# One core, three chained layers: the right-hand tiles of the last layer begin 352 bytes lower

## The chip, the cores and the metric

The kernel runs on one core of one Trainium2 chip. The metric is the device time of one execution in microseconds. All times below are of the kernel before the change.

## The reference

Three layers follow one another. The first is attention with the delta rule (4 batches, 8 heads, 768 tokens, head size 48): a state of 48x48 for each head is read and updated token by token. Its output, turned to 3072 tokens by 384, goes through two feed-forward layers. What matters here is the last one.

```
def _moe_ref(x, w_in, w_out):            # layer 1: 384 -> 2048 -> 384
    h = np.maximum(x @ w_in, 0.0)
    return h * h @ w_out
def _moe2_ref(x, w_gate, w_val, w_out):  # layer 2: 384 -> 1536 -> 384
    gate = 1.0 / (1.0 + np.exp(-(x @ w_gate)))
    val = x @ w_val
    return gate * val @ w_out
```

All data are 32-bit floats. The kernel keeps the precision with split operands: each number is a high part and a low part, and each product is three matmuls (high x high, low weight x high, high weight x low).

## The kernel before, in words

**Order of the work.** Attention and layer 1 are interleaved by a list of steps written out by hand (`ORDER`); every engine runs its instructions in the order in which the program issues them, and the framework adds the waits. Layer 1 makes `h` from `xhi`, `xlo` with the weights `w1h` (high, kept in SBUF) and `il` (low, fetched for each step) in line 681, and adds to `o` in line 719 with `gh`, `gl`. The tokens go in six groups of 512 columns, so the matmuls of both layers have 128 rows, 128 weights and 512 columns.

**Layer 2.** Three pairs of groups are handled together by a scheme that needs fewer products (11 instead of 12 for a pair of groups and a pair of hidden blocks). For each pair there are 12 halves: six pairs of hidden blocks, each for `gate` and for `val`. One half has seven pieces (`PIECES`), each of three or six matmuls that add up in one PSUM tile `gx` or `gy` (line 1138). Their weights come from `wg`; their moving operands are ten blocks of tokens or of sums of tokens: three of them lie in `xhi`, `xlo`, seven in `xa` (first and third pair) or `xb` (second pair). VectorE adds every piece to `gateA` to `gateD` or `valA` to `valD` (line 1052), ScalarE copies the first piece (line 1142) and takes the sigmoid, and VectorE multiplies `gate` by `val` (line 1063). The products are split into `gh`, `gl` (or `p` tiles), and their matmuls with `wo` into `o` (line 1019) are put between the pieces. The last group's output is made at the end in line 1197, with the hidden values as weights and `wo` as the moving operand, 384 columns.

**What is prepared on the way.** During the end of layer 1 and the first pair, VectorE, ScalarE and GpSimd convert raw weights (`raw2`, `y2`, lines 792 to 809), make sums of weights (`wr`, line 859) and split them into `wg` (lines 867, 872) and `wo` (lines 880, 884); token sums come from `x2r` and `xt` (lines 914 to 926).

**Where the tiles lie.** SBUF is given out from two sides. On the left lie `work` (`xhi`, `xlo`, `gg`, `gh`, `gl`, `p`), the weights of layer 1 and, once these are closed, `w2y`: eight of the twelve blocks of `wo` (f from 4 to 11), `xb`, `obt`, and the `gate` and `val` tiles. All of these begin at 128 modulo 512 bytes of the partition. On the right lay the tiles of attention; when they are closed, the pool `w2x` takes their place: `xa`, `x2r`, `xt`, `raw2`, `y2`, the first four blocks of `wo`, and `wr`, `wor`, `wg`. A pool on the right ends at the top of SBUF and its tiles lie upward from its base in the order in which they are made. A column slice of a moving operand is 2048 bytes and one of the weights 512 bytes, and the tiles are multiples of 512 bytes, so every operand of layer 2 has the place modulo 512 of the tile that it is in.

Of the kernel before, what the change touches and what calls it, by code (L numbers as in the profile page):

```python
# [7 lines left out]
F32 = mybir.dt.float32  # L8
# [83 lines left out]
def kernel(  # L92
# [681 lines left out]
    with tc.manual_schedule():  # L774
# [39 lines left out]
        assert not (z_t or kn_t or v_t or q_t or pm_t or N_t or xr_t or yt_t or o_t)  # L814
        at.close()
        w2x = ctx.enter_context(tc.tile_pool(name="w2x", bufs=1, side="right", reuse_waits="tile"))
        w2x.tile([128, 24], F32, name="pad")
        xa_t = w2x.tile([128, 2, 7, GT], F32R, name="xa")
        x2r_t = w2x.tile([128, 2, KD, GT], F32, tag="x2r", name="x2r")
        xt_t = w2x.tile([128, GT], F32, name="xt")  # L820
# [189 lines left out]
        def o_product(g, f, m, i, start, stop):  # L1010
            if start:
                po2[g, m] = (
                    ps_o.tile([128, GT], F32, tag=f"o{m}", name=f"o{m}") if g % 2 == 0
                    else ps_2.tile([128, GT], F32, tag=f"o{m + 3}", name=f"o{m + 3}")
                )
            hi, lo = (w[:, m * 128:m * 128 + 128] for w in wo_t[f])
            ph, pl = p_t[g, f]
            w, x = ((hi, ph), (lo, ph), (hi, pl))[i]
            nc.tensor.matmul(out=po2[g, m], lhsT=w, rhs=x, start=start, stop=stop)  # L1019
# [60 lines left out]
        for hh in range(halves):  # L1080
# [87 lines left out]
            if v:  # L1168
                assert not queue
                for k, (g, f) in enumerate(((g0, fo), (g0, fe), (g0 + 1, fe), (g0 + 1, fo))[:4 if g0 + 2 < NG else 2]):  # L1170
                    for m in range(KD):
                        for r in range(3):
                            queue.append([
                                lambda g=g, f=f, m=m, r=r, a=j == 0 and k % 2 == 0 and r == 0, z=j == NP - 1 and k % 2 and r == 2:
                                o_product(g, f, m, r, bool(a), bool(z)), None])
                    if j == NP - 1 and k % 2:
                        queue[-1][1] = g
        while after:
            k = min(after)
            for fn in after.pop(k):  # L1180
                step[0] = k
                fn()
# [114 lines left out]
```

## Time and profile before

| | |
|---|---|
| median of three runs | 1065.0 us |
| the three runs | 1072.24, 1065.0, 1062.05 us |
| the profiled execution | 1069.8 us, span 1068.1 us |
| granted TensorE clock, mean over the span | 0.99 |
| first matmul of layer 2 (line 1138) | 632.9 us |
| last matmul of line 1138 and line 1019 | 1033.5 and 1038.2 us |
| last stage (line 1197) | 1038.5 to 1063.8 us |

The span runs from the first to the last instruction; the time of the execution has 1.7 us more around it. Layer 2 and the last stage take the last 435 us of it. The number after the duration of a matmul in a row is its count; matmuls overlap, so their distance from start to start is shorter than their duration.

### The profile page before, as it was taken

Reading aid. Unit: us, or ns where it says so; the run is one execution under the profiler, and the core shown is the slowest. Engines: PE = TensorE matmul, PEld = TensorE weight load, DVE = VectorE, ACT = ScalarE, POOL = GpSimd, SP = SyncE. Lnnn points to the kernel's source line nnn. Section 1 sums busy time; section 2 is a strip of 40 time slices with the busy share of each in tenths; the row PEclk is TensorE's granted clock in tenths of the full one; section 3 lists DMA queues with packets and bytes.
Section 4 is the critical chain, followed back from the end, with each engine's and each line's share of the span. In section 5 each row is a group of like instructions: output and inputs, shape, how many; then the busy total and the mean of one; then the engine's idle time right before and its main releaser. Section 6 shows DMA issues by size and latency. Waiting matters only on the chain.

```text
span 1068.1 us, 27414 instructions
## 1 busy us (share of the span) xinstructions
PE 1001.8 (94%) x11611; PEld 819.5 (77%) x11611; DVE 763.3 (71%) x1436; ACT 458.4 (43%) x763; POOL 233.9 (22%) x181
## 2 busy tenths in 40 slices
PE   4575999999999999999999999999999999999998
PEld 2564777777787887788788887787888888878888
DVE  6979889868788874974344768988676566676770
ACT  2343665454554555445555745434322332222220
POOL 4352444200011101010011015668601221000000
PEclk9998999999999999999999999999999999999999
DMA  9666666675685856665547766644644332244302
GB/s 268 187 211 171 219 200 196 215 201 148 166 217 146 243 169 197 173 187 174 149 150 248 245 214 242 219 157 149 231 144 133 102 121 88 91 135 160 117 1 60
DMA packets 81803, 182.78 MB, mean 171 GB/s; under 512 B 22032, under 2 KB 54928, under 8 KB 77072
## 3 DMA queue, kind: packets, MB, share of 16 engines
q1 hardware_dynamic: 81392, 180.76, 55.2%
q8 instruction: 91, 1.49, 0.6%
q10 hardware_dynamic: 288, 0.26, 0.1%
q14 instruction: 32, 0.26, 0.1%
HBM read 139.30 MB, written 36.96 MB: 165 GB/s over the span
## 4 chain that ended last, share of the span: by engine, by line
PE 82%; DVE 4%; DMA 4%; issue 2%; SPq 1%; ACT 1%; DVEq 0%; ACTq 0%
PE h L681 17%; PE o L719 17%; PE gx L1138 12%; PE gy L1138 12%; PE o L1019 11%; PE r L1197 2%; DMA il<-w1d 2%; PE att L553 1%; PE att L584 1%; PE att L620 1%; PE att L622 1%; PE att L566 1%; PE att L377 1%; PE att L538 1%; PE att L363 1%
## 5 line engine op out<-in xcount | busy, mean ns | idle before, releaser
L704 DVE TENSOR_TENSOR gl<-gg,gh 128x512 fp32r<-128x512 f32 x96 | 72.8, 765 | 88.4 <-ACT gg L698 87.9
L695 ACT ACTIVATE gg<-h 128x512 f32<-128x512 f32 x96 | 57.4, 598 | 177.8 <-PE h L681 170.8
L719 PE MATMUL o<-gh,il 128*128 128x512 f32 x288 | 112.7, 391 | 1.0 <-DMA il<-w1d 1.0
L1019 PE MATMUL o<-gh,wo 128*128 128x512 f32 x270 | 93.1, 395 | 0.0
L681 PE MATMUL h<-xhi,il 128*128 128x512 f32 x288 | 84.5, 402 | 4.6 <-issue 2.7
L719 PE MATMUL o<-gh,w1h 128*128 128x512 f32 x216 | 86.9, 402 | 0.0
L719 PE MATMUL o<-gl,w1h 128*128 128x512 f32 x216 | 84.3, 390 | 0.0
L1138 PE MATMUL gy<-xa,wg 128*128 128x512 f32 x288 | 76.4, 394 | 0.3
L1138 PE MATMUL gx<-xa,wg 128*128 128x512 f32 x288 | 76.5, 394 | 0.0
L681 PEld LDWEIGHTS h<-xhi,il 128*128 128x128 f32 x288 | 55.3, 193 | 18.6 <-issue 3.6
L168 POOL TENSOR_TENSOR y<-raw 128x768 f32<-128x768 f32 x12 | 19.7, 1644 | 220.1 <-DVE raw L161 195.7
L681 PE MATMUL h<-xhi,w1h 128*128 128x512 f32 x216 | 65.7, 413 | 0.0
L1138 PEld LDWEIGHTS gy<-xa,wg 128*128 128x128 f32 x288 | 53.9, 188 | 13.5 <-DVE gateB L1052 0.6
L1138 PEld LDWEIGHTS gx<-xa,wg 128*128 128x128 f32 x288 | 53.9, 188 | 13.2 <-DVE gateB L1052 0.5
L719 PEld LDWEIGHTS o<-gh,il 128*128 128x128 f32 x288 | 54.1, 188 | 12.3 <-DMA il<-w1d 1.9
L681 PE MATMUL h<-xlo,w1h 128*128 128x512 f32 x216 | 62.4, 398 | 0.0
L698 ACT ACTIVATE gg<-gg 128x512 f32<-128x512 f32 x96 | 60.7, 632 | 3.1
L697 ACT ACTIVATE gh<-gg 128x512 fp32r<-128x512 f32 x96 | 60.7, 632 | 3.1
L1019 PEld LDWEIGHTS o<-gh,wo 128*128 128x128 f32 x270 | 50.7, 188 | 11.9
L1019 PE MATMUL o<-gl,wo 128*128 128x512 f32 x135 | 53.1, 393 | 0.0
L463 DVE TENSOR_TENSOR tmp<-xi,tt 128x40 f32<-128x40 f32 (+7 forms) x208 | 50.7, 277 | 1.3
L470 DVE TENSOR_TENSOR tt<-tt,tmp 128x40 f32<-128x40 f32 (+7 forms) x208 | 50.5, 275 | 1.5 <-DVE tmp L463 0.2
(232 smaller groups left out, 2268.3 us busy)
## 6 DMA issues: line engine op xcount, KB each, us to landing
il<-w1d SPq DMA_DIRECT2D x192, 192.0 KB, 3.5
wg<-wgd SPq DMA_DIRECT2D x24, 1152.0 KB, 5.3
raw<-in_w_dram SPq DMA_DIRECT2D x19, 768.0 KB, 4.9
wgd<-wg SPq DMA_DIRECT2D x12, 1152.0 KB, 6.1
w1s<-in_w_dram SPq DMA_DIRECT2D x9, 768.0 KB, 5.5
w1d<-wl SPq DMA_DIRECT2D x16, 384.0 KB, 4.2
kz<-in_kz_dram SPq DMA_DIRECT2D x32, 192.0 KB, 5.7
kn<-in_kn_dram SPq DMA_DIRECT2D x12, 384.0 KB, 4.9
```

The lines of the kernel that those rows point to most:

```text
L168: nc.gpsimd.tensor_tensor(out=t, in0=c["t"], in1=c["raw"][:, :, 0].bitcast(F32), op=ALU.add)
L463: nc.vector.tensor_tensor(out=tv[i], in0=xi[:, 0:j, j].unsqueeze(2).to_broadcast([128, j, n]), in1=tt[:, j, lo:hi].unsqueeze(1).to_broadca ...
L470: nc.vector.tensor_tensor(out=tt[:, 0:j, lo:hi], in0=tt[:, 0:j, lo:hi], in1=tv[i], op=ALU.subtract)
L681: nc.tensor.matmul(out=ps[:, cs], lhsT=w[:, kc * 128:kc * 128 + 128], rhs=x[:, kc, cs], start=(i == 0 and kc == 0), stop=(i == 2 and kc == ...
L695: nc.scalar.activation(out=gg, in_=ps, func=ACTF.Relu)
L697: nc.scalar.activation(out=gh, in_=gg, func=ACTF.Square)
L698: nc.scalar.activation(out=gg, in_=gg, func=ACTF.Square)
L704: nc.vector.tensor_tensor(out=gl, in0=gg, in1=gh.bitcast(F32), op=ALU.subtract)
L719: nc.tensor.matmul(out=po[m], lhsT=w[:, cs], rhs=x, start=(f == 0 and i == 0), stop=(f == NF1 - 1 and i == 2),)
L1019: nc.tensor.matmul(out=po2[g, m], lhsT=w, rhs=x, start=start, stop=stop)
L1138: nc.tensor.matmul(out=ps, lhsT=a, rhs=c, start=k == 0 and u == us[0], stop=k == 2 and u == us[-1],)
L1197: nc.tensor.matmul(out=po_m, lhsT=x[:, cs], rhs=w, start=f == 0 and i == 0, stop=f == NF2 - 1 and i == 2)
```

## The change

A filler of 24 numbers (96 bytes) at the base of `w2x` goes, and a filler of 88 numbers (352 bytes) is made as the last tile of the pool. The pool is thus 256 bytes longer, its base lies 256 bytes lower, and its tiles lose the 96 bytes in front of them: all lie 352 bytes lower. They began at 480 modulo 512 and now begin at 128 modulo 512. No instruction is added, removed or moved in the program's order. Fillers are never written or read.

```
         w2x = ctx.enter_context(tc.tile_pool(name="w2x", bufs=1, side="right", reuse_waits="tile"))
-        w2x.tile([128, 24], F32, name="pad")
         xa_t = w2x.tile([128, 2, 7, GT], F32R, name="xa")
...
                     if j == NP - 1 and k % 2:
                         queue[-1][1] = g
+        w2x.tile([128, 88], F32, name="pad")
         while after:
             k = min(after)
```

## Rows read from the trace of the kernel before

**Rows 1.** The page: busy engines, then shares of the chain of waits by line.

```profile
PE 1001.8 (94%) x11611; PEld 819.5 (77%) x11611; DVE 763.3 (71%) x1436; ACT 458.4 (43%) x763; POOL 233.9 (22%) x181
...
PE h L681 17%; PE o L719 17%; PE gx L1138 12%; PE gy L1138 12%; PE o L1019 11%; PE r L1197 2%; DMA il<-w1d 2%; PE att L553 1%; PE att L584 1%; PE att L620 1%; PE att L622 1%; PE att L566 1%; PE att L377 1%; PE att L538 1%; PE att L363 1%
```

**Rows 2.** Groups by line on PE, 570 to 632 us: count, busy us, mean ns.

```profile
L719 PE MATMUL o<-gh,il 128*128 128x512 f32 x47 | 18.3, 389 | 0.0
...
L681 PE MATMUL h<-xhi,il 128*128 128x512 f32 x45 | 12.6, 389 | 0.0
```

**Rows 3.** Groups by line on PE, 636 to 647 us, the start of layer 2.

```profile
L1138 PE MATMUL gx<-xa,wg 128*128 128x512 f32 x21 | 5.4, 389 | 0.0
...
L1138 PE MATMUL gy<-xhi,wg 128*128 128x512 f32 x4 | 1.3, 395 | 0.0
L1138 PE MATMUL gy<-xlo,wg 128*128 128x512 f32 x2 | 0.8, 395 | 0.0
```

**Rows 4.** Groups by line on PE, 800 to 835 us, the second pair.

```profile
L1019 PE MATMUL o<-gh,wo 128*128 128x512 f32 x30 | 10.3, 396 | 0.0
L1138 PE MATMUL gx<-xb,wg 128*128 128x512 f32 x36 | 9.6, 396 | 0.0
```

**Rows 5.** Groups by line on PE, 1037 to 1064 us, the last stage.

```profile
L1197 PE MATMUL r<-wo,xb 128*128 128x384 f32 x72 | 13.3, 337 | 0.0
L1197 PE MATMUL r<-wo,px 128*128 128x384 f32 x36 | 6.9, 337 | 0.0
L1197 PE MATMUL r<-wo,phi 128*128 128x384 f32 x24 | 6.1, 334 | 0.0
```

**Rows 6.** Windows: length, PE busy (records touching the window), granted clock, DMA.

```profile
570.00:630.00 60.00, 60.00 (x267) 1.00 0.75 239
662.00:692.00 30.00, 30.00 (x131) 1.00 0.69 220
694.00:727.00 33.00, 33.00 (x144) 1.00 0.51 172
735.00:835.00 100.00, 100.00 (x431) 1.00 0.47 154
835.00:935.00 100.00, 100.00 (x432) 1.00 0.28 96
948.00:1035.00 87.00, 87.00 (x378) 1.00 0.32 106
```

**Rows 7.** Windows, all engines: PE, PEld, DVE, ACT, POOL busy.

```profile
649.00:709.00 60.00, 59.41 (x255) 47.60 (x255) 52.60 (x94) 24.01 (x42) 37.48 (x28) 1.00 0.60 201
...
835.00:910.00 75.00, 75.00 (x325) 60.63 (x324) 47.23 (x72) 21.36 (x39) 15.49 (x11) 1.00 0.28 95
```

**Rows 8.** Waits of PE, 632 to 1039 us: total us, times, longest.

```profile
PE gx L1138 <- DVE valC L1052: 1.4, 1, 1.4
PE gy L1138 <- DVE gateC L1052: 0.4, 1, 0.4
```

**Rows 9.** Timeline around 730 us, start and length: weight sums on VectorE.

```profile
729.55 3.25 DVE L859 TENSOR_TENSOR wr<-wr 128x128 f32<-128x128 f32 x4
...
733.46 0.73 PE L1138 MATMUL gy<-xhi,wg 128*128 128x512 f32 x2 [0.40 <-DVE gateC L1052]
```

**Rows 10.** Tiles xa and xb on VectorE: ns min/median/max, first and last start.

```profile
L926 DVE TENSOR_TENSOR xa<-xt,xa x3: 681/686/693, 592.9 to 619.9; 128x512 fp32r<-128x512 f32 x3
...
L1071 DVE TENSOR_TENSOR xb<-valB,xb x3: 681/684/684, 936.2 to 976.9; 128x512 fp32r<-128x512 f32 x3
```

**Rows 11.** The page's DMA issues: count, KB each, us to landing.

```profile
x2r<-x2d SPq DMA_DIRECT2D x6, 768.0 KB, 6.8
```

**Rows 12.** First and last start: attention's n and tmp; then y2's writers.

```profile
L553 PE MATMUL att<-n,xi x768: 191/191/258, 51.2 to 534.6; 32*32 32x32 f32 x192
...
L463 DVE TENSOR_TENSOR tmp<-xi,tt x208: 161/260/1957, 167.8 to 500.8; 128x21 f32<-128x21 f32 x8, 128x40 f32<-128x40 f32 x8, 128x57 f32<-128x57 f32 x8, 128x72 f32<-128x72 f32 x8
...
L794 DVE TENSOR_SCALAR y<-raw x12: 347/352/358, 584.6 to 702.6; 128x384 uint32<-128x384 uint32 x12
```

More of the change, by code (lines that the diff above doesn't have):

```diff
@@ L816 @@
         w2x = ctx.enter_context(tc.tile_pool(name="w2x", bufs=1, side="right", reuse_waits="tile"))
-        w2x.tile([128, 24], F32, name="pad")
         xa_t = w2x.tile([128, 2, 7, GT], F32R, name="xa")
@@ L1177 @@
                         queue[-1][1] = g
+        w2x.tile([128, 88], F32, name="pad")
         while after:
```

## The prediction

> **What bounds the kernel now.** I read the page first. TensorE (PE) is busy for 1001.8 of 1068.1 us, and in the chain of waits the three matmul lines of layer 2 hold 12%, 12% and 11% of the span, the last stage 2% [rows 1]. So from 632.9 us on the time is the number of matmuls times their distance from start to start, plus a few waits. The waits of PE next, for the stretch of layer 2: the longest is 1.4 us and the next 0.4 us, both on VectorE's additions [rows 8]; in 402 us that is nothing. What is left to ask is why one matmul takes as long as it does.
>
> For that I took the groups by line in stretches where the same shape (128x512, split operands, granted clock 1.00, which is the level of 2.4 GHz) works with tiles of different places. Layer 1 at its end has all operands on the left: 389 ns [rows 2]. At the start of layer 2, products of `xa` with `wg`, both on the right, take 389 ns as well, while in the same microseconds `xhi` and `xlo` from the left with `wg` from the right take 395 [rows 3]. In the second pair everything is mixed: `xb`, `xhi` and `gh` are on the left, `wg` and the first blocks of `wo` on the right, and every group takes 396 ns [rows 4]. The last stage says it a third time with other shapes: `phi` with a `wo` block of the left takes 334 ns, `px` (right) with a left block and `xb` (left) with mostly right blocks 337 [rows 5]. So the row that is slower isn't that of a line, a tile or a side; it is the one whose moving operand and weights (or the weights of the next matmul, loaded during this one) lie at different places modulo 512, here 128 and 480. Both at 128 or both at 480 cost the same.
>
> How much time is that? A window that PE fills gives the distance: its length by the records that begin in it. The count of a window has about 389/227 = 1.7 records too many, those that were running at its edge. Layer 1: 60 us by 265.3 is 226.2 ns, and one record more or less makes it 0.9 ns other. The five windows of layer 2 without waits have 1516 records, 1507.5 without the edges, in 350 us: 232.2 ns; single windows go from 231 to 233 [rows 6]. The difference is 6.0 ns with an uncertainty of 0.9. The durations give from 0 to 7 ns by stretch [rows 2 to 4]. I take 5.5 ns.
>
> **The change part by part.** Nothing is added to or removed from any engine's program; what moves is the place of the right-hand tiles, from 480 to 128 modulo 512. Every slice of them moves alike.
>
> *Matmuls of layer 2.* Lines 1138 and 1019 have 1188 and 540 matmuls: per half 33 for gate or val, 36 halves; 3 x 3 for each hidden block and group, 12 blocks, five groups. With all operands at 128 they are in the situation of layer 1, so 1728 x 5.5 ns = 9.5 us goes. At the start of layer 2 the products of `xa` are already without the excess [rows 3], 21 of `gx` and about as many of `gy`: 42 x 5.5 ns = 0.2 us less, 9.3. As bounds I take 1728 x 5.1 = 8.8 and 1728 x 6.9 = 11.9 us, less the same 0.2.
>
> *Last stage.* 72 matmuls with `xb` and 36 with `px` lose 3 ns each [rows 5]: 0.3 us. Together 9.6 us.
>
> *What it meets.* The saved time is on the path only where PE stays the last. From 835 to 910 us VectorE is busy for 47 of 75 us, and 9.6 us spread over 400 us shortens a piece between two uses of a PSUM tile by some 30 ns. There it is all kept. From 649 to 709 us VectorE is busy for 52.6 of 60 us [rows 7], because weight sums and conversions come on top and are held up beside GpSimd: four sums took 3.25 us, and behind them an addition came too late and PE stood for 0.40 us [rows 9]. If VectorE were the bound in that stretch, its share of the gain, 255 x 5.5 ns = 1.4 us, would be lost; if it never is, nothing. I take 0.5 us, near the lower end, since PE has only waits of 1.4 and 0.4 us so far.
>
> *Waits.* The new places lie on other tiles of attention by 352 bytes: `y2` now begins on `n`, and the second `wg` on the end of `tmp`, so their first writers wait for the last readers of these too. Those began at 534.6 and 500.8 us; the first write into `y2` is at 584.6 us [rows 12], and `wg` is first written five steps later in the order. Nothing is queued behind these waits, since they are over by some 50 us. Cost 0. If one did hold, VectorE's step after it and all conversions would shift; nothing in the rows points to it.
>
> *Transfers.* The trace can't show a right-hand tile at 128. The largest, `x2r`, lands in 6.8 us [rows 11] while PE works on; the one wait that could hang on it is the 1.4 us one [rows 8]. So between 1.4 us less and 1.4 us more, and I take 0, as the row names VectorE and not a transfer.
>
> *VectorE itself.* Its subtraction with output and inputs on the right takes 686 ns, on the left 684 [rows 10]. Cost 0; from both sides 2 ns on some 60 such operations, 0.1 us.
>
> The page "SBUF — State Buffer" of the Trainium skill, section "A bandwidth-pool intuition that's wrong (but worth ruling out)", speaks against all this: it gives the loading of weights a second, independent read port beside that of the moving operand, so the place of one should be nothing to the other. By that the sum would be 0 and the time 1065. [Rows 3] and [rows 4] differ by 7 ns for one shape at one clock, which that rule alone does not give.
>
> The sum: 9.3 + 0.3 - 0.5 = 9.1 us. The profiled execution took 1069.8 us (span 1068.1 and 1.7 around it), so it would be 1060.7; it stood 4.8 us over the median of the three runs, and its surplus can't be told from layer 2. Taken off the median, 1065.0 - 9.1 = 1055.9 us, in round numbers 1056.
>
> **The rivals.**
>
> *The place isn't the cause: same time.* Layer 2 differs from layer 1 in more than places: VectorE reads PSUM all the time (line 1052), and `o` and `g` matmuls alternate between tiles. If that makes the 5.5 ns, nothing changes: 1065.0, within the 3 us by which the lower two runs differ. Against it stands that `xa` with `wg` is at 389 ns among the same neighbours [rows 3], and `phi` at 334 inside one loop with `xb` at 337 [rows 5]. For it: those two stretches are short, and in the first VectorE has fewer additions behind it. The rule of the second port, quoted above, would have this outcome. Chance 0.12. That the tiles don't come to lie where the change says, say by 96 or 256 bytes instead of 352, gives the same time, since the places would still differ: 0.03.
>
> *Half is given back in the first pair.* VectorE becomes the bound from 649 to 770 us: 517 matmuls x 5.5 ns = 2.8 us are lost, and three new waits of the kind of the 0.40 us one [rows 9] add 1.2 us. 1065.0 - 9.6 + 4.0 = 1059.4. For it speaks the load of 88% [rows 7], against it that the waits are few [rows 8]. Chance 0.12.
>
> *Slower, by weight sums that fall badly.* The sums of line 859 run once in each of the eight halves from 649 us to 740; if a faster PE brings every one of them beside a GpSimd operation, as in [rows 9], the addition behind it comes late, and a full miss costs what the longest wait does, 1.4 us, plus the 0.4 us of the next one [rows 8]. Eight of these are 14.4 us: 1065.0 - 9.6 + 14.4 = 1069.8. It decides from the sixth on. Against it: the halves have these sums already, and two waits of that size are all that came of it. Chance 0.03.
>
> **How the numbers follow.** Forecast 1056.0 us with chance 0.70; its own range is 1053 to 1059 from the bounds (8.8 to 11.9 us, 0 to 1.4 lost, 1.4 either way for transfers). No effect 0.15 (both forms), half given back 0.12, slower 0.03. The runs before lie between 1062.05 and 1072.24, so within 1% (10.65 us) this kernel's measurement can hardly tell a change from none. The range reaches from 1052.0, the forecast's lower end less one for scatter, to 1063.0, which takes in the rival at 1059.4 and the near part of no effect. Faster by over 1% would need a gain above 10.65 us, which only the upper bound of the excess gives: a third of 0.70, 0.24. Slower by over 1%, above 1075.65, only if the slower rival comes out worse than priced or the scatter goes against me: 0.03. Within 1%: 0.73.
>
> **What would show each step.** In the profile after, the groups of lines 1138 and 1019 should read 389 ns in every stretch, the window from 835 to 935 us should hold about 442 records instead of 432, and `xb` and `px` in line 1197 should read 334. Layer 1 and attention should be as before to within the scatter. If line 1138 stays at 394 to 396 ns, the place isn't the cause. If the durations fall and the first matmul of line 1197 still comes some 405 us after the first of line 1138, the gain went into waits on VectorE, to be seen in the list of PE's waits between 649 and 770 us. What makes the prediction wrong beyond that is a finer dependence on the place (modulo 1024, say), which layer 1's rows would have averaged away.

## The result and the profile after

| | before | after |
|---|---|---|
| median | 1065.3 us (9 runs, 1062.05 to 1072.24) | 1056.3 us (9 runs, 1053.05 to 1063.55) |
| ratio | | 0.991, 95% interval 0.9881 to 0.994 |
| profiled execution (span) | 1069.8 us (1068.1) | 1056.1 us (1054.3) |
| first matmul of layer 2 | 632.9 us | 627.2 us |
| first matmul of line 1197 | 1038.5 us | 1024.9 us |
| between these two | 405.6 us | 397.7 us |

The median is 9.0 us lower, with 6.4 to 12.7 us from the interval. That is less than the 10.2 us by which single runs of the old kernel differ, but the interval leaves out zero. The two profiled executions differ by more, 13.8 us, and they show where: 5.7 us are gone before layer 2 begins; 7.9 us in layer 2; 0.2 us in the last stage. Of the first part, 5.2 us are gone by 181 us from the start, long before the first tile of `w2x` is written, so it is scatter; a later run of the old kernel has scatter in the same place (below). The change's own part is thus 8.1 us. With the filler moved, lines of the layer 2 loop have numbers one lower in the changed kernel (1138 is 1137, 1052 is 1051, 1019 is 1018); line 1197 keeps its number.

The groups by line on PE from 630 to 641 us, which answer to [rows 3]; the columns are count, busy us and mean ns:

```profile
L1137 PE MATMUL gx<-xa,wg 128*128 128x512 f32 x22 | 5.8, 389 | 0.0
...
L1137 PE MATMUL gy<-xhi,wg 128*128 128x512 f32 x4 | 1.2, 389 | 0.0
L1137 PE MATMUL gy<-xlo,wg 128*128 128x512 f32 x2 | 0.8, 389 | 0.0
```

The same view from 788 to 823 us, in the second pair, for [rows 4]:

```profile
L1018 PE MATMUL o<-gh,wo 128*128 128x512 f32 x31 | 10.4, 389 | 0.0
L1137 PE MATMUL gy<-xb,wg 128*128 128x512 f32 x39 | 10.2, 391 | 0.0
L1137 PE MATMUL gx<-xb,wg 128*128 128x512 f32 x35 | 9.2, 389 | 0.0
```

And the last stage, 1024.5 to 1050 us, for [rows 5]:

```profile
L1197 PE MATMUL r<-wo,xb 128*128 128x384 f32 x72 | 13.1, 334 | 0.0
L1197 PE MATMUL r<-wo,px 128*128 128x384 f32 x36 | 6.9, 334 | 0.0
```

What was 395 or 396 ns in those rows is 389 in both stretches, and `xb` and `px` went from 337 to 334. (The 391 is one matmul of 445 ns in that window.) The windows of [rows 6] read, as length, PE busy with its records, clock and transfers:

```profile
735.00:835.00 100.00, 100.00 (x443) 1.00 0.50 166
835.00:935.00 100.00, 99.24 (x434) 1.00 0.30 101
948.00:1025.00 77.00, 77.00 (x340) 1.00 0.30 99
```

443 records in 100 us instead of 431: 100 / 441.3 is 226.6 ns, the distance of layer 1. The window from 835 to 935 us holds only 434, because waits that came at 939 to 947 us before now begin at 927 us, inside it. Ahead of them, in 75 us that PE fills, there are 333 records (x after the second number) instead of the 325 of [rows 7], so the distance is 226.4 ns:

```profile
829.00:904.00 75.00, 75.00 (x333) 62.10 (x332) 48.00 (x73) 22.33 (x40) 12.49 (x9) 1.00 0.32 109
```

The waits of PE from 620 to 1039 us (total us, times, longest), for [rows 8]:

```profile
PE gx L1137 <- DVE valC L1051: 1.5, 1, 1.5
PE gy L1137 <- DVE gateC L1051: 1.0, 2, 0.8
PE gy L1137 <- DVE gateD L1051: 0.3, 1, 0.3
PE gy L1137 <- DVE gateB L1051: 0.2, 1, 0.2
```

They grew from 2.1 us to 3.0. The 2.1 us are [rows 8] and this row of the kernel before:

```profile
PE gy L1138 <- DVE gateD L1052: 0.3, 1, 0.3
```

Most of the growth is in the stretch behind the weight sums, as the timeline (start and length) shows beside [rows 9]:

```profile
722.46 3.53 DVE L858 TENSOR_TENSOR wr<-wr 128x128 f32<-128x128 f32 x4
...
726.64 0.73 PE L1137 MATMUL gy<-xhi,wg 128*128 128x512 f32 x2 [0.79 <-DVE gateC L1051]
```

Counted another way, all distances from start to start over 260 ns in layer 2 held 4.5 us beyond 227 ns before (17 of them) and 5.7 us after (20). The rest of the distances had a mean of 232.1 ns before and 226.9 after. 1711 x 5.3 = 9.0 us less in distances, 1.1 us more in waits, makes 7.9.

### The profile page after: what moved, and what is told of

It reads as the page before. It is cut to its first block, busy times and chain, and to the rows that moved or that the text cites. A ratio compares the mean times of both kernels' runs of the same rounds, so it can differ in the third digit from the quotient of the medians.

```text
span 1054.3 us, 27410 instructions
## 1 busy us (share of the span) xinstructions
PE 989.0 (94%) x11607; PEld 817.0 (77%) x11611; DVE 763.9 (72%) x1436; ACT 458.3 (43%) x763; POOL 234.3 (22%) x181
## 4 chain that ended last, share of the span: by engine, by line
PE 85%; DMA 2%; DVE 2%; issue 2%; SPq 1%; ACT 1%; DVEq 0%; ACTq 0%
PE h L681 19%; PE o L719 18%; PE gx L1137 12%; PE gy L1137 12%; PE o L1018 11%; PE r L1197 2%; DMA il<-w1d 2%; PE att L620 1%; PE att L553 1%; PE att L538 1%; PE att L584 1%; PE att L566 1%; PE att L622 1%; PE att L377 1%; PE att L363 1%
```

## The experiments

The theory: while PE streams the moving operand of one matmul it loads the weights of the next; if the two lie at different places modulo some power of two (512 in the prediction), the matmul takes longer. Rivals: 480 is simply a worse place than 128; a matmul's own two operands decide; or something else in layer 2 makes the excess. The measure is mostly the time from the first matmul of layer 2 to the first of line 1197, which I call the length of layer 2, read from one profile each; how far that can be trusted is the last experiment.

**All tiles at 480.** The kernel before, with the left side moved up to the place of the right instead of the right side down:

```
     const = ctx.enter_context(tc.tile_pool(name="const", bufs=1))
+    const.tile([128, 88], F32, name="pad0")
...
-        w2x.tile([128, 24], F32, name="pad")
```

> The kernel before with the filler of w2x removed and a filler of 352 bytes at the base of the left side: every left tile moves up to 480 modulo 512, where the right tiles of layer 2 already are. Theory (the distance between moving operand and weights decides, not the place itself): matmuls of layer 2 at 389 ns as in the changed kernel, first matmul of layer 2 to first of line 1197 about 398 us instead of 405.6, median 1056 +- 3 us. Rival (480 is the worse place, 128 the better one): 395 to 397 ns in every stretch, layer 1 too, layer 2 at 405 us or more, and layer 1 slower by up to 1728 x 5 ns = 9 us, so 1065 to 1075 us.

Median 1055.0 us (4 runs), ratio 0.9909 to the kernel before, interval 0.9873 to 0.9944. The length of layer 2 is 397.7 us again. Groups by line from 570 to 625 us (layer 1; its lines are one higher here), and from 790 to 825 us:

```profile
L682 PE MATMUL h<-xhi,il 128*128 128x512 f32 x39 | 10.9, 389 | 0.0
...
L1138 PE MATMUL gx<-xb,wg 128*128 128x512 f32 x35 | 9.2, 389 | 0.0
```

At 480, layer 1 is as quick as at 128, and layer 2 is as quick as in the changed kernel. The place itself is nothing; only the distance between the sides counted. The first rival is out.

**The matmuls alone.** This kernel computes none of the reference. It has one moving tile, weights at different distances behind it, and 24 matmuls for each distance. In the measured groups VectorE and GpSimd are idle and ScalarE only copies PSUM at the end of each. Four more groups alternate places 0 and 352 in the moving operand, in the weights or in both. The core of it:

```
    for d in (0, 16, 32, 64, 96, 128, 192, 256, 320, 352, 384, 448, 480, 496):
        w = wt(at(d, 384, f"w{d}b"))
        work.append([(A[i % 2], w[i % 3]) for i in range(24)])
    for name, flip_m, flip_w in (("own", 0, 1), ("next", 0, 0), ("wts", None, 0), ("mov", 0, None)):
        ...
        pick = lambda i, flip: 0 if flip is None else (i + flip) % 2
        work.append([(m[pick(i, flip_m)][i // 2 % 2], w[pick(i, flip_w)][i // 2 % 3]) for i in range(24)])
```

> Computes none of the reference: 120 matmuls of 128x512 to begin with, then groups of 24 with weights at 0, 16, 32, 64, 96, 128, 192, 256, 320, 352, 384, 448, 480 and 496 bytes modulo 512 behind the moving operand, then four groups that alternate places 0 and 352: own (each matmul's own weights at the other place, the next matmul's weights at the place of this one's moving operand), next (own weights at the same place, the next ones at the other), wts (only weights alternate), mov (only the moving operand alternates). No other engine works meanwhile. Theory (loading the next weights meets the streaming of this moving operand): 227 ns from start to start at distance 0, and at 352 about 234; group own at 227, group next at 234 or near it. Rival (a matmul's own two operands decide): own at 234, next at 227. Rival (other engines' work in layer 2 makes the excess): 227 everywhere. For the other distances no theory has a figure beforehand; 227 at 256 would say that 256 is the period.

The groups by tile: duration min/median/max in ns, first and last start in us. The number in the weights' name is the distance in bytes:

```profile
L143 PE MATMUL p<-m,w0b x24: 389/389/389, 33.7 to 38.9; 128*128 128x512 f32 x24
...
L143 PE MATMUL p<-m,w16b x24: 389/389/397, 39.2 to 44.4; 128*128 128x512 f32 x24
...
L143 PE MATMUL p<-m,w32b x24: 392/395/397, 44.6 to 50.0; 128*128 128x512 f32 x24
...
L143 PE MATMUL p<-m,w192b x24: 388/392/397, 67.0 to 72.3; 128*128 128x512 f32 x24
...
L143 PE MATMUL p<-m,w256b x24: 388/389/395, 72.5 to 77.7; 128*128 128x512 f32 x24
...
L143 PE MATMUL p<-m,w352b x24: 391/396/400, 83.6 to 89.0; 128*128 128x512 f32 x24
...
L143 PE MATMUL p<-mnextB,wnextB x12: 392/398/401, 117.1 to 122.3; 128*128 128x512 f32 x12
...
L143 PE MATMUL p<-mownB,wownA x12: 390/397/397, 111.6 to 116.7; 128*128 128x512 f32 x12
...
L143 PE MATMUL p<-mownA,wownB x12: 387/387/390, 111.4 to 116.4; 128*128 128x512 f32 x12
```

From start to start, averaged over the starts of each group in the trace:

| distance, bytes | 0 | 16 | 32 | 64 | 96 | 128 | 192 | 256 | 320 | 352 | 384 | 448 | 480 | 496 |
|---|---|---|---|---|---|---|---|---|---|---|---|---|---|---|
| ns | 226.7 | 226.7 | 233.1 | 233.4 | 233.9 | 233.5 | 228.9 | 227.2 | 233.4 | 233.9 | 233.5 | 228.9 | 233.3 | 229.1 |

The excess is there with nothing else at work, so the third rival is out. 64 and 320, 96 and 352, 128 and 384, 192 and 448 are pairs to 0.1 ns, and 256 is as good as 0: the period is 256 bytes, not 512. Most distances cost 6.4 to 7.2 ns, 192, 448 and 496 cost 2.2 to 2.4, 16 nothing. Group next had 234.0 ns, own 229.7, with alternating 224 and 236; wts and mov, where every second load is at the other place, 230.3 each. That is the mean of 226.7 and 234, but single distances there alternate between 229 and 231, not between 227 and 234. So the load of the next weights beside the stream counts for more than a matmul's own weights: 7.3 ns over the floor in next, 3.0 in own. The excess in own, where every load agrees with the stream that it begins under, was not foreseen, and it means that the theory is not the whole of it. One reading, not tested, is that a load reaches past the change from one stream to the next.

**Distance 256 in the kernel.** The changed kernel with its filler split, 256 bytes at the base and 96 at the end:

```
+        w2x.tile([128, 64], F32, name="pad0")
         xa_t = w2x.tile([128, 2, 7, GT], F32R, name="xa")
...
-        w2x.tile([128, 88], F32, name="pad")
+        w2x.tile([128, 24], F32, name="pad")
```

> The changed kernel with 256 bytes of its end filler moved to the base of w2x: right tiles at 384 modulo 512, that is 256 from the left ones. Theory with a period of 512: excess as in the kernel before, layer 2 at 403 to 407 us, 1065 +- 3 us. Same theory with a period of 256 (or 128): 389 ns, 398 us, 1056 us. Rival (the start within 64 bytes decides: 128 and 384 are multiples of 64, 480 isn't): 389 ns, 398 us, 1056 us as well; e2 tells these two apart.

Median 1058.2 us (10 runs), ratio 0.9932, interval 0.9908 to 0.9957; length of layer 2 397.7 us (629.7 to 1027.4). Groups by line, 790 to 825 us:

```profile
L1019 PE MATMUL o<-gh,wo 128*128 128x512 f32 x30 | 10.0, 389 | 0.0
...
L1138 PE MATMUL gx<-xb,wg 128*128 128x512 f32 x36 | 9.5, 389 | 0.0
```

The period is 256 in the kernel too. By itself this would also fit the rival of starts within 64 bytes; but the distances 64, 128, 320 and 384 cost the full price in the matmuls alone, so that is out.

**Distances 192 and 32 in the kernel.** The same edit with 48 and 40 numbers as fillers (192 bytes at the base), and with 8 and 80 (32 bytes).

> The changed kernel with 192 bytes at the base of w2x and 160 at its end: right tiles at 320 modulo 512, 192 from the left ones. Alone, distance 192 gave 228.9 ns and 352 gave 233.9 against 226.7. Theory (the excess is that of the distance modulo 256, diluted as in the kernel before, where 7.2 ns alone became 5.5 ns over all of layer 2): 2.2 ns alone becomes 1.7 ns, 1728 of these are 2.9 us, so first matmul of layer 2 to first of line 1197 about 400.5 us. Rival (aligned or not, with one price): 405 us.

> The changed kernel with 32 bytes at the base of w2x and 320 at its end: right tiles at 160 modulo 512, 32 from the left ones. Alone, distance 32 gave 233.1 ns, 6.4 over 226.7. Theory: 4.9 ns over layer 2, 8.4 us, so 404 to 405 us from the first matmul of layer 2 to the first of line 1197. Rival (a small distance costs little): 398 to 400 us.

One profile each. Groups by line from 792 to 827 us, of the kernel with 192:

```profile
L1138 PE MATMUL gx<-xb,wg 128*128 128x512 f32 x36 | 9.5, 392 | 0.0
```

and with 32:

```profile
L1138 PE MATMUL gx<-xb,wg 128*128 128x512 f32 x34 | 9.2, 396 | 0.0
```

With 32 bytes the length of layer 2 is 404.8 us (628.6 to 1033.5), as expected: a slip of 32 bytes costs nearly all that 352 did. With 192 it is 401.9 us (631.3 to 1033.1), between the theory's 400.5 and the rival's 405. The price is graded, but I had it too small: the mean distance in layer 2 was 229.7 ns, 3.1 over the floor instead of 1.7. One reason is the direction: weights on the left behind a moving operand on the right are 64 away modulo 256, and that costs 6.7 ns and not 2.2. This can hold only where a matmul with `wo` follows one of `xa`; there are 110 such places, and they hold 0.35 us of the excess.

The largest share, 1.8 us, lies where no operand differs: 461 matmuls of `xa` whose own and next weights are both in `wg`, on the same side, took 230.9 ns from start to start and 226.9 in the changed kernel. They had an excess in the kernel before too, 230.7 ns, which the rows from the start of layer 2 do not show. A row from the third pair (1007 to 1014 us) does:

```profile
L1138 PE MATMUL gx<-xa,wg 128*128 128x512 f32 x12 | 3.1, 392 | 0.0
```

So the excess spreads to neighbours. In the kernel before, the first five matmuls of a run of `xa` had means of 232.3, 231.8, 231.0, 230.1 and 228.5 ns, and from the sixth on 226.5 to 227. Only two runs are longer than six, both at the start of layer 2, and [rows 3] come from these. Why a matmul whose operands agree still pays behind others that don't, no run here shows.

**Attention's tiles moved too.** The 352 bytes at the top of the right side, so that attention's tiles move with the rest:

```
+    top = ctx.enter_context(tc.tile_pool(name="top", bufs=1, side="right"))
+    top.tile([128, 88], F32, name="pad")
...
-        w2x.tile([128, 88], F32, name="pad")
```

> The changed kernel with the 352 bytes at the top of the right side instead of the end of w2x, so that the tiles of attention lie 352 bytes lower too, most of them at 128 modulo 512 like the left. Layer 2 as in the changed kernel (397.7 us). Theory: in the first 627 us the 128x512 matmuls of layer 1 have only 1.5 us of excess outside waits in the profile, next to small ones of attention, so at most 1 to 2 us is gained: 1055 +- 3 us. Rival (attention's own small matmuls and its DVE work gain too, or the place costs them): 1045 to 1050 us, or over 1060.

Median 1055.6 us (6 runs), ratio 0.9914, interval 0.9887 to 0.9941; length of layer 2 397.7 us (629.9 to 1027.6). The gain of 1 to 2 us, if there is one, can't be seen; a gain or loss of 5 us or more is out.

**Where the weight sums stand.** The waits that grew come behind these sums. In three variants of the changed kernel the sums of the gate halves are issued one piece earlier, one later, or two and two:

```
-        WP0, WP1, WLE = (2, 4, 6, 5, 6), (2, 1, 4, 3, 5), (nc.gpsimd, nc.gpsimd)
+        WP0, WP1, WLE = (2, 3, 6, 5, 6), (2, 1, 4, 3, 5), (nc.gpsimd, nc.gpsimd)   # earlier
+        WP0, WP1, WLE = (2, 5, 6, 5, 6), (2, 1, 4, 3, 5), (nc.gpsimd, nc.gpsimd)   # later
...
+        WP0, WP1, WLE = (2, 4, 6, 5, 6, 5), (2, 1, 4, 3, 5, 1), (nc.gpsimd, nc.gpsimd)   # split
```

> The changed kernel with the weight sums of the gate halves issued one piece earlier (piece 3 instead of 4). Theory (the waits that grew by 1.1 us come from VectorE being late behind these sums when GpSimd works beside them): the wait of 1.2 us around 725 us goes or shrinks, layer 2 shorter by 0.3 to 1.2 us than 397.7. Rival (the waits come from the load of VectorE as a whole, wherever the sums stand): 397.7 +- 0.3 us, with a wait of like size elsewhere between 645 and 770 us.

> The changed kernel with the weight sums of the gate halves issued one piece later (piece 5 instead of 4). One piece earlier made PE wait 6 us more, so the sums' place against GpSimd's subtractions decides. Theory (a place where GpSimd is done with its subtraction frees VectorE): layer 2 at 396 to 397.5 us, the wait of 1.2 us at 725 us gone. Rival (piece 4 is the only gap, any other place delays an addition): 399 to 405 us.

> The changed kernel with the four weight sums of the gate halves in two parts, two after piece 4 and two after piece 5. Theory (waits of PE come from VectorE held for 3.5 us in one go): layer 2 at 396 to 397.5 us. Rival (each part is held up by GpSimd as the whole was): 398 us or more.

The split one also has `w_sums` make two of the four sums at a time. All three are longer than 397.7 us: 404.0 earlier, 399.7 later, 398.5 split, one profile each. What I expected was wrong in sign for all three. The first one's waits of PE (total us, times, longest):

```profile
PE gx L1137 <- DVE gateB L1051: 6.3, 4, 3.1
```

and its timeline before the longest of them:

```profile
728.09 4.91 DVE L858 TENSOR_TENSOR wr<-wr 128x128 f32<-128x128 f32 x4
...
734.37 0.96 PE L1137 MATMUL gx<-xa,wg 128*128 128x512 f32 x3 [3.08 <-DVE gateB L1051]
```

In the other two the wait on `gateC` at 726 us is gone, as expected, but the one on `valC` grew, in the later and in the split kernel:

```profile
PE gx L1137 <- DVE valC L1051: 2.3, 2, 1.8
...
PE gx L1138 <- DVE valC L1051: 2.1, 2, 1.6
```

So the waits do hang on the sums and where they fall (one piece earlier costs 6.3 us, one later 2.0), but the place after piece 4 is the best of the four tried, and the 1.1 us could not be had back this way. The kernel before shows what stretches the sums: one takes 276 to 294 ns while GpSimd does nothing, and each that overlaps a GpSimd instruction takes longer by about the overlap (1544 ns with 1398 of overlap). The row of all of them (min/median/max):

```profile
L859 DVE TENSOR_TENSOR wr<-wr x48: 276/285/1544, 606.2 to 737.5; 128x128 f32<-128x128 f32 x48
```

**The kernel before once more.**

> The kernel before, unchanged, for the scatter of one profile against another. Theory (the 630 us ahead of layer 2 differ from execution to execution and layer 2 does not): first matmul of layer 2 between 627 and 633 us, from there to the first of line 1197 405.6 +- 0.2 us. Rival (layer 2 itself differs by microseconds between executions): 400 to 410 us there, so that one profile's difference of 7.9 us means little.

The first matmul of layer 2, in the row of its tile (min/median/max ns, first and last start):

```profile
L1138 PE MATMUL gx<-xhi,wg x108: 388/394/498, 634.9 to 1027.9; 128*128 128x512 f32 x108
```

and the first of line 1197:

```profile
L1197 PE MATMUL r<-wo,xb x72: 334/338/343, 1040.5 to 1062.4; 128*128 128x384 f32 x72
```

Length 405.6 us, the same as in the first profile. The part ahead was 2 us longer, 634.9 us, above the range that I gave; the eleven profiles of full kernels lie between 627.2 and 634.9 us there. This execution took 1071.8 us and another of the same program in the same session 1062.3. Layer 2 repeats to 0.1 us, and also 397.7 came four times (changed kernel, all at 480, distance 256, attention too). One profile is enough to compare it; whole times need many runs.

## Why the prediction was right

*What bounds the kernel.* Right. The gain came out of the distance between matmuls in a stage that PE fills.

*Matmuls of layer 2.* Right: the distance fell to that of layer 1 in every stretch. Predicted 9.3 us, measured 9.0. The step of 5.5 ns was 5.3. The window that was to show it from 835 to 935 us, about 442 records, read 434: the distance was as expected, but waits had moved into the window.

*The place as the cause.* That it is the relation between weights and moving operand was right (all at 480 does as well), and the next weights count for most of it. The modulus was too strict: 256 does. And the prediction took a matmul whose operands agree to be free of the excess, from rows at the start of layer 2; for most such matmuls of the kernel before that was not so (230.7 ns against 226.9). The sum didn't suffer, because its 5.5 ns came from windows over all matmuls.

*Last stage.* Predicted 0.3 us, measured 0.2.

*What is lost to waits.* The stretch and the mechanism were right, VectorE late behind weight sums; the size was low: 0.5 us predicted, 1.1 measured, within its bounds of 0 and 1.4. Some 0.8 us of it lies between 643 and 727 us, with 0.4 at the wait on `gateC` alone; the rest lies at 789, 927 to 935 and 1023 us, which I had not named.

*Waits on attention's tiles, transfers, VectorE.* Priced at 0, and nothing contradicts it: in layer 2 no wait of PE on a transfer is in the list, and the first matmul of layer 2 came no later than before.

*The sum.* 9.1 us predicted. The profiles give 8.1, the medians 9.0 with an interval of 6.4 to 12.7; that these agree so well with 1056.0 is partly luck, since the interval is 6.3 us wide.

*The rivals.* That the place isn't the cause, or that the tiles don't lie where the change says, fell with the rows at 389 ns. The rule of the page "SBUF — State Buffer" of the Trainium skill, section "A bandwidth-pool intuition that's wrong (but worth ruling out)", that the load of weights has a second, independent read port, does not cover what the matmuls alone show: 233.9 instead of 226.7 ns when the two lie 352 bytes apart. The other two rivals would have shown 4 us or more of new waits; there were 1.1.

## What to carry to other kernels

When PE is the bound, compare the duration of one matmul shape between stages of the same kernel; 389 against 396 ns for the same work pointed to the operands' places. Lay all operands of a stream of matmuls at the same place modulo 256 bytes of the partition: here, for matmuls of 128x512, a slip of 32 bytes cost 2.8% of the distance from one to the next alone and 2.0% in layer 2, and a filler of a few hundred bytes repaired it. A gain on PE is paid out in full only where the engines that feed it have slack; read their load by stage first.

## What was not expected of the hardware

The period is 256 bytes, and the price is not the same for all distances: 16 and 256 bytes cost 0.5 ns or less, 192, 448 and 496 2.2 to 2.4 ns, the others tried 6.4 to 7.2 ns for a 128x512 matmul of 226.7 ns, at a granted clock of 1.00. It does not end where the places agree again, but up to five matmuls later. The weight loads themselves read 187 or 188 ns in the median at every distance. In the kernel before, single distances ran from 231 to 238 ns where both places were mixed (around 805 us), not a constant 234. And four small sums on VectorE took 3.5 us or 4.9 us in one piece or another of the same loop; a move to one piece earlier made 6 us of waits.
